# A convolution and two feed-forward layers in one kernel: layer 2 begins behind four blocks of layer 1, its weights are split at an even pace, TensorE's row halves start at unit 16

## The chip, the cores and the metric

The kernel runs on one core of a Trainium2 chip. Its time is the device time of one execution in microseconds (us). Before the change it is 2398.25 us, the median of three runs (2397.28 to 2398.75).

## What is computed

The inputs are x of 4 x 4096 x 192 (16384 tokens of 192 channels), 8 x 7 filter taps, and two pairs of weights, w_in of 192 x 2048 and w_out of 2048 x 192. The reference, cut to what matters:

```python
w = softmax(weight)                                   # 8 heads, 7 taps, each head 24 channels
x = causal convolution of x with w, head by head      # 16384 x 192
h = np.maximum(x @ moe_w_in, 0.0);  x = h * h @ moe_w_out                    # layer 1
h = x @ moe2_w_in
g = np.where(h > 0.0, h, np.exp(np.minimum(h, 0.0)) - 1.0);  out = g @ moe2_w_out   # layer 2
```

The weights arrive as 64-bit words (the kernel reads each as two 32-bit halves, `raw[..., 0]` and `raw[..., 1]`, and builds a float from them).

## The kernel before, in words

**Precision by splitting.** TensorE multiplies in a reduced format (float32r). So each operand, weights, inputs and the hidden values g, is held as a high part and a low part, and each product is three: high by high, low by high, high by low.

**Blocks and units.** Tokens are cut into 32 blocks of 512 (`NB`, `TB`). The 2048 hidden columns are 16 tiles of 128, taken two at a time: 8 pairs (`NP`). One *unit* is one layer, one block, one pair: 512 units in all. In the program's loop over u, TensorE does for unit u the products of x with w_in (`gemm1`, into the PSUM tile `h`), and for unit u - 3 (`LAG`) those of g with w_out (`gemm2`, into the PSUM tiles `y1A`, `y1B` or `y2A`, `y2B`). Between the two stand, for each unit: `r`, the relu of h by ScalarE (`act_first`); in layer 2 an exponential by ScalarE and then an operation of VectorE; the square in layer 1, by ScalarE up to unit 39; `gh`, the high part, by ScalarE (`finish_g`); `gl`, the low part, by VectorE or for five units by GpSimd (`finish_lo`).

**192 channels.** They are 128 ("A") and 64 ("B"). The B part of x fills only 64 of 128 rows, so the tokens' two halves lie in the two row halves, and each half of B is copied to the other row half as well (`move`, four DMAs a block, into `x1Bh` and `x1Bl`), since both halves of the array need it.

**Two ways of multiplying.** Before unit `HALVES` (32) a product is one instruction over 128 rows. From there on (`products` with halves) it is two instructions over 64 rows each, issued in pairs, half 0 and half 1 with different work, so that the two run together. The halves write to the same PSUM tile at different times, and SyncE's queue carries the signals between them (the no-operations in `products`, `SIGNALS` and `WAITS`): in this stage whatever is issued on that queue stands between signals, and so `later` puts a DMA off by two units.

**Order of the units.** `merge` interleaves block 0 of layer 1 with block 1, shifted by 3 units (units 0 to 15). Then block 2 of layer 1 is interleaved with block 0 of layer 2 (units 16 to 31). From unit 32 on come whole blocks: layer 2 block 1, layer 1 block 3, layer 2 block 2, layer 1 block 4, and so on.

**The weights in pieces.** Each layer's weights are cut into 18 pieces (`pieces`: six of A, four of B, eight of w_out, "o"), each with a unit at which it is due. `piece_step` works on three pieces at once: it ends an old one (`finish`: a copy by ScalarE or GpSimd and subtractions by GpSimd), begins a new one (`start`, `sign`, `guard`: a Square by ScalarE and three operations by VectorE), and does the middle of one (`power`, `rest`: two by VectorE, an addition by GpSimd), and then loads a further one by DMA into `raw`. So a step is five operations on VectorE. `more_pieces` makes up to two steps in a unit, as long as the piece is due within 8 units (4 for the last pieces), and `pieces_for` those that are due now. Each engine runs its instructions in program order, so a step stands on VectorE between one unit's `gl` and the next one's.

**The x side.** For each block `place_tasks` transposes x in, and `conv_tasks` applies 7 taps to the A part (`acc`, 128x512) and 7 to the B part (128x256) on VectorE, then splits the result (`hi_a`, `hi_b` on ScalarE, `lo_a`, `lo_b` on VectorE). For blocks 0 and 1 ("early") the B taps are ScalarE multiplications added up by GpSimd. These tasks wait in the list `bg`, which gives two or more to each unit; where a unit's block is not ready, the loop `while (layer, j) not in ready` takes all that is left at once.

Of the kernel before, what the change touches and what calls it, by code (L numbers as in the profile page):

```python
# [8 lines left out]
F32 = mybir.dt.float32  # L9
# [7 lines left out]
P = 128  # L17
TB = 512
# [4 lines left out]

LEAD = 3

HALVES = 32

AHEAD = (8, 4)

A_PIECES = ((0, 2), (2, 4), (4, 7), (7, 10), (10, 13), (13, 16))  # L30
B_PIECES = ((0, 2), (2, 4), (4, 6), (6, 8))
# [4 lines left out]
def f32(ap):  # L36
    return ap.bitcast(F32)
# [3 lines left out]
def conv_moe_moe_kernel(  # L41
# [34 lines left out]
    xt_p = ctx.enter_context(tc.tile_pool(name="xt", bufs=2))  # L76
    acc_p = ctx.enter_context(tc.tile_pool(name="acc", bufs=1))
    in_p = ctx.enter_context(tc.tile_pool(name="in", bufs=2))
    tmp_p = ctx.enter_context(tc.tile_pool(name="tmp", bufs=3))
    g_p = ctx.enter_context(tc.tile_pool(name="g", bufs=LAG))  # L80
    ev_p = ctx.enter_context(tc.tile_pool(name="ev", bufs=2))
    ps_h = ctx.enter_context(tc.tile_pool(name="ps_h", bufs=2, space=PSUM))
    ps_1 = ctx.enter_context(tc.tile_pool(name="ps_1", bufs=2, space=PSUM))
    ps_2 = ctx.enter_context(tc.tile_pool(name="ps_2", bufs=2, space=PSUM))


    cwA = cpool.tile([P, K], F32, name="cwA")
# [55 lines left out]
    class Piece:  # L143


        def __init__(self, layer, part, c0, c1):
            self.layer, self.part, self.c0, self.c1 = layer, part, c0, c1
            self.n = (c1 - c0) * (D if part == "o" else P)

        def load(self):  # L150
            wi, wo = w32[2 * (self.layer - 1) : 2 * self.layer]
# [166 lines left out]
    def conv_tasks(j, early=False):  # L318
        tasks = []
        st = {}  # L320

        def tap(i, cw, k):
            t = xT[j][i]
            n = (TB, HB)[i]
            if early and i == 1:
                c = acc_p.tile([P, n], F32, tag="acc1" if k == 0 else "tap", name="acc", bufs=1 if k == 0 else 2)
                nc.scalar.mul(out=c, in_=t[:, k : k + n], mul=cw[:, k : k + 1])
                if k == 0:
                    st[i] = c
                else:  # L330
                    nc.gpsimd.tensor_tensor(out=st[i], in0=st[i], in1=c, op=ALU.add)
            elif k == 0:
                st[i] = acc_p.tile([P, n], F32, tag=f"acc{i}", name="acc")
                nc.vector.tensor_scalar(out=st[i], in0=t[:, 0:n], scalar1=cw[:, 0:1], scalar2=None, op0=ALU.mult)
            else:
                nc.vector.scalar_tensor_tensor(  # L336
                    out=st[i], in0=t[:, k : k + n], scalar=cw[:, k : k + 1], in1=st[i], op0=ALU.mult, op1=ALU.add
                )

        def hi_a():  # L340
            X1[j] = in_tiles("x1")
            nc.scalar.copy(out=X1[j][0], in_=st[0])

        def lo_a():
            eng = nc.gpsimd if j in (1, 2) else nc.vector
            eng.tensor_tensor(out=X1[j][1], in0=st[0], in1=f32(X1[j][0]), op=ALU.subtract)

        def halves():
            return [(slice(s * DB, (s + 1) * DB), slice(s * HB, (s + 1) * HB)) for s in range(2)]

        def hi_b():
            for p, n in halves():
                nc.scalar.copy(out=X1[j][2][p, n], in_=st[1][p, :])

        def lo_b():
            h, l = X1[j][2:]
            for p, n in halves():
                nc.vector.tensor_tensor(out=l[p, n], in0=st[1][p, :], in1=f32(h[p, n]), op=ALU.subtract)


            def move(t, p, n, other):
                nc.sync.dma_start(out=f32(t[other, n]), in_=f32(t[p, n]))
                if t is l and other.start == 0:
                    ready.add((1, j))

            for t in (h, l):
                for (p, n), (other, _) in zip(halves(), reversed(halves())):
                    later(lambda t=t, p=p, n=n, other=other: move(t, p, n, other))

        for k in range(K):  # L370
            tasks.append(lambda k=k: tap(0, cwA, k))
            tasks.append(lambda k=k: tap(1, cwB, k))
        return tasks + [hi_a, hi_b, lo_a, lo_b]
# [19 lines left out]

    Y = {}

    def gemm2(layer, j, i, gh, gl):

        if i == 0:
            pool, tag = (ps_1, "y1") if layer == 1 and j != 1 else (ps_2, "y2")
            Y[layer, j] = [pool.tile([P, TB], F32, tag=tag, name=f"y{layer}{s}") for s in "AB"]  # L400
        o = (W1 if layer == 1 else W2)["o"]
        hi, lo, b = slice(0, P), slice(D + DB, 2 * D), slice(P, D + DB)
        todo = {
            "A": [(s, d, g) for s in range(2) for d, g in ((hi, gh), (lo, gh))] + [(s, hi, gl) for s in range(2)],
            "B": [(s, b, g) for g in (gh, gl) for s in range(2)],
        }
        work = {}
        for half in range(2):
            for y, part in zip(Y[layer, j], "AB"):
                begins = i == 0 and half == "AB".index(part)  # L410
                ends = i == NP - 1 and half != "AB".index(part)
                last = len(todo[part]) - 1
                work[half, part] = [
                    (o[:, 2 * i + s, d], g[:, s, :], y, begins and k == 0, ends and k == last)
                    for k, (s, d, g) in enumerate(todo[part])
                ]
        return work
# [57 lines left out]
    def fold_b(yB, n):  # L475

        t = ev_p.tile([P, TB], F32, tag="yt", name="yt", bufs=1)
        for d in range(0, n, DB):
            nc.scalar.copy(out=t[d : d + DB, :], in_=yB[DB - d : P - d, :])
        s = ev_p.tile([P, TB], F32, tag="ys", name="ys", bufs=1)  # L480
        nc.vector.tensor_tensor(out=s[0:n], in0=yB[0:n], in1=t[0:n], op=ALU.add)
        return s

    def y1_tasks(j):
        st = {}

        def split_to(hi, lo, src):
            nc.scalar.copy(out=hi, in_=src)
            nc.vector.tensor_tensor(out=lo, in0=src, in1=f32(hi), op=ALU.subtract)

        def a():
            X2[j] = in_tiles("x2")
            st["s"] = fold_b(Y[1, j][1], P)

        def b():
            split_to(X2[j][0], X2[j][1], Y.pop((1, j))[0])

        def c():
            split_to(X2[j][2], X2[j][3], st["s"])
            ready.add((2, j))  # L500

        return [a, b, c]

    def y2_tasks(j):

# [23 lines left out]
        return [unit for _, _, unit in sorted(at)]  # L529

    units = merge((1, 0, 0, 1.0), (1, 1, LEAD, 1.0))
    first_l2 = len(units)
    units += merge((1, 2, 0, 1.0), (2, 0, 0, 0.85))
    for j in range(3, NB):
        units += [(layer, b, c) for layer, b in ((2, j - 2), (1, j)) for c in range(NP)]
    units += [(2, j, c) for j in (NB - 2, NB - 1) for c in range(NP)]
    NU = len(units)
    at = {unit: u for u, unit in enumerate(units)}

    due, queue = zip(*(pieces(1) + pieces(2)))  # L540
    n_loaded = n_piece = 0

    def load_piece():
        nonlocal n_loaded
        if n_loaded < len(queue):
            queue[n_loaded].load()
            n_loaded += 1

    def piece_step():

        nonlocal n_piece
        i = n_piece
        new, mid, old = (queue[k] if 0 <= k < len(queue) else None for k in (i, i - 1, i - 2))
        if old:
            old.finish()
        if new:
            new.start()
        if mid:
            mid.power()
        if new:  # L560
            new.sign()
        if mid:
            mid.rest()
            load_piece()
        if new:
            new.guard()
        n_piece += 1
# [4 lines left out]
            piece_step()  # L572

    def more_pieces(u):
        ahead = AHEAD[n_piece >= len(queue) - 8]
        if n_piece < len(due) + 2 and due[max(n_piece - 2, 0)] <= u + ahead:
            piece_step()

    with tc.manual_schedule():
# [44 lines left out]
        def next_x(l2, j2, c2):  # L624

            if (l2, j2) == (1, 1):
                return {0: 2, 6: 3}.get(c2)
            if l2 == 2 and j2 and c2 == 2 and j2 + 3 < NB:
                return j2 + 3

        for u in range(NU + LAG):
            now = u
            pieces_for(u)
            if u < NU:
                layer, j, c = units[u]
                while (layer, j) not in ready:
                    bg.popleft()[1]() if bg else transfer()
                hs[u], first = gemm1(W1 if layer == 1 else W2, (X1 if layer == 1 else X2)[j], c)
# [22 lines left out]
            if 0 <= v:  # L661
                l2, j2, c2 = units[v]
                if c2 == NP - 1:
                    tasks = (y1_tasks if l2 == 1 else y2_tasks)(j2)
                    if v < first_l2 or (l2, 0) in [(n[0], n[2]) for n in units[v + 1 : v + 3]]:
                        for t in tasks:
                            t()
                    else:
                        bg.extendleft((0, t) for t in reversed(tasks))
                jx = next_x(l2, j2, c2)  # L670
                if jx:

# [42 lines left out]
```

## Time and profile before

| | |
|---|---|
| median of three runs | 2398.25 us |
| the profiled execution, its own time | 2400.75 us |
| its span, first to last instruction | 2399.0 us |
| mean granted TensorE clock, share of full | 0.988 |
| TensorE busy with matmuls | 2315.8 us (97%) |
| VectorE busy | 1746.5 us (73%) |
| ScalarE busy | 1489.1 us (62%) |
| GpSimd busy | 126.9 us (5%) |

The profile's 40 slices of the span are 60 us each. TensorE's busy share in tenths is 4, 7, 7, 8 in the first four and 9 in all that follow but the last (7). The granted clock is 8 or 9 tenths in the first four. GpSimd is busy in these four alone. TensorE's chain of matmuls makes up 82% of the chain that ended last. So the page has two parts: some 240 us in which TensorE waits now and then, and 2140 us in which it hardly does.

In the trace a unit is found by its first matmul into `h`. Unit 0's begins at 22.02 us, unit 16's at 136.62; unit 32, the first in halves, begins at 239.99.

### The profile page before, as it was taken

Reading aid. Unit: us, or ns where it says so; the run is one execution under the profiler, and the core shown is the slowest. Engines: PE = TensorE matmul, PEld = TensorE weight load, DVE = VectorE, ACT = ScalarE, POOL = GpSimd, SP = SyncE. Lnnn points to the kernel's source line nnn. Section 1 sums busy time; section 2 is a strip of 40 time slices with the busy share of each in tenths; the row PEclk is TensorE's granted clock in tenths of the full one; section 3 lists DMA queues with packets and bytes.
Section 4 is the critical chain, followed back from the end, with each engine's and each line's share of the span. In section 5 each row is a group of like instructions: output and inputs, shape, how many; then the busy total and the mean of one; then the engine's idle time right before and its main releaser. Section 6 shows DMA issues by size and latency. Waiting matters only on the chain.

```text
span 2399.0 us, 45460 instructions
## 1 busy us (share of the span) xinstructions
PE 2315.8 (97%) x18948; PEld 1935.1 (81%) x18948; DVE 1746.5 (73%) x2053; ACT 1489.1 (62%) x1641; POOL 126.9 (5%) x132
## 2 busy tenths in 40 slices
PE   4778999999999999999999999999999999999997
PEld 2555888888888888888888888888888889888886
DVE  7978677777777777777777777777777777777654
ACT  4656666656666656666666666665666666666664
POOL 5546000000000000000000000000000000000000
PEclk8989999999999999999999999999999999999998
DMA  3311100101000110100010100010010001010000
GB/s 87 85 48 42 16 16 13 19 16 17 17 15 13 18 18 16 19 12 15 16 19 15 19 15 15 13 19 17 17 18 13 14 17 19 14 19 5 12 8 14
DMA packets 222621, 49.08 MB, mean 20 GB/s; under 512 B 206545, under 2 KB 220881, under 8 KB 222417
## 3 DMA queue, kind: packets, MB, share of 16 engines
q1 hardware_dynamic: 221312, 46.05, 10.0%
q8 instruction: 150, 2.46, 0.4%
q14 instruction: 55, 0.44, 0.1%
q10 hardware_dynamic: 1104, 0.13, 0.1%
HBM read 25.17 MB, written 12.58 MB: 16 GB/s over the span
## 4 chain that ended last, share of the span: by engine, by line
PE 82%; DVE 8%; ACT 5%; issue 2%; SPq 1%; DMA 1%; POOL 0%; DVEq 0%; ACTq 0%
PE h L435 38%; PE y2A L435 13%; PE y1A L435 13%; PE y1B L435 8%; PE y2B L435 8%; ACT gh L611 2%; DVE r L471 2%; ACT r L458 1%; DVE gl L617 1%; DVE acc L336 1%; ACT r L462 1%; DVE a L176 1%; SPq L513 1%; DVE r L469 1%; DVE a L187 0%
## 5 line engine op out<-in xcount | busy, mean ns | idle before, releaser
L611 ACT CAST gh<-r 128x1024 fp32r<-128x1024 f32 x512 | 537.5, 1050 | 632.1 <-DVE r L469 322.5
L617 DVE TENSOR_TENSOR gl<-r,gh 128x1024 fp32r<-128x1024 f32 x507 | 625.9, 1235 | 339.1 <-ACT gh L611 339.1
L458 ACT ACTIVATE r<-h 128x1024 f32<-128x1024 f32 x512 | 524.1, 1024 | 180.3 <-PE h L435 155.7
L435 PE MATMUL y2A<-gh,wo 64*128 64x512 f32 x1968 | 539.2, 393 | 8.4 <-issue 7.6
L435 PE MATMUL y1A<-gh,wo 64*128 64x512 f32 x1872 | 511.7, 392 | 0.9 <-SPq L440 0.7
L471 DVE SCALAR_TENSOR_TENSOR r<-r,h 128x1024 f32<-128x1024 f32 x256 | 311.7, 1218 | 239.1 <-ACT r L462 216.4
L435 PEld LDWEIGHTS y2A<-gh,wo 64*128 64x128 f32 x1968 | 356.5, 185 | 39.1 <-issue 8.4
L435 PEld LDWEIGHTS y1A<-gh,wo 64*128 64x128 f32 x1872 | 338.0, 184 | 26.0 <-SPq L440 4.0
L469 DVE SCALAR_TENSOR_TENSOR r<-h,r 128x1024 f32<-128x1024 f32 x232 | 282.6, 1218 | 48.4 <-ACT r L458 47.8
L435 PE MATMUL h<-x2Ah,wiAh 64*128 64x512 f32 x992 | 311.6, 394 | 0.0
L435 PE MATMUL h<-x2Ah,wiAl 64*128 64x512 f32 x992 | 310.4, 392 | 0.0
L435 PE MATMUL h<-x2Al,wiAh 64*128 64x512 f32 x992 | 310.4, 393 | 0.0
L435 PE MATMUL y2A<-gl,wo 64*128 64x512 f32 x984 | 309.4, 394 | 0.0
L435 PE MATMUL y2B<-gh,wo 64*128 64x512 f32 x984 | 308.4, 393 | 0.0
L435 PE MATMUL y2B<-gl,wo 64*128 64x512 f32 x984 | 308.1, 392 | 0.0
L435 PE MATMUL y1B<-gl,wo 64*128 64x512 f32 x936 | 292.7, 392 | 0.3 <-DVE gl L617 0.3
L435 PE MATMUL y1B<-gh,wo 64*128 64x512 f32 x936 | 292.6, 392 | 0.0
L435 PE MATMUL y1A<-gl,wo 64*128 64x512 f32 x936 | 292.6, 392 | 0.0
L435 PE MATMUL h<-x1Ah,wiAl 64*128 64x512 f32 x928 | 290.1, 392 | 0.0
L435 PE MATMUL h<-x1Al,wiAh 64*128 64x512 f32 x928 | 290.0, 392 | 0.0
L435 PE MATMUL h<-x1Ah,wiAh 64*128 64x512 f32 x928 | 290.0, 392 | 0.0
L462 ACT ACTIVATE r<-r 128x1024 f32<-128x1024 f32 x256 | 271.5, 1061 | 7.8
(126 smaller groups left out, 4862.6 us busy)
## 6 DMA issues: line engine op xcount, KB each, us to landing
xinA<-in_x_dram SPq DMA_DIRECT2D x128, 64.0 KB, 2.3
out_dram<-zA SPq DMA_DIRECT2D x128, 64.0 KB, 2.0
raw<-in_moe_w_out_dram SPq DMA_DIRECT2D x16, 384.0 KB, 3.2
x1Bh<-x1Bh SPq DMA_DIRECT2D x64, 64.0 KB, 2.0
x1Bl<-x1Bl SPq DMA_DIRECT2D x64, 64.0 KB, 2.0
out_dram<-zB SPq DMA_DIRECT2D x64, 64.0 KB, 2.0
xinB<-in_x_dram SPq DMA_DIRECT2D x124, 32.0 KB, 2.0
raw<-in_moe_w_in_dram SPq DMA_DIRECT2D x8, 384.0 KB, 3.3
```

Of the source, the lines that this page charges most:

```text
L176: nc.vector.tensor_scalar(out=self.a.bitcast(U32), in0=hw, scalar1=3, scalar2=0x3FFFFFFF, op0=ALU.logical_shift_left, op1=ALU.bitwise_and,)
L336: nc.vector.scalar_tensor_tensor(out=st[i], in0=t[:, k : k + n], scalar=cw[:, k : k + 1], in1=st[i], op0=ALU.mult, op1=ALU.add)
L435: m = nc.tensor.matmul(o, w[p], x[p], start=st, stop=sp)
L458: nc.scalar.activation(out=r, in_=h, func=AF.Relu, scale=1.0 if layer == 1 else -1.0)
L462: nc.scalar.activation(out=r, in_=r, func=AF.Exp, scale=-1.0)
L469: nc.vector.scalar_tensor_tensor(out=r, in0=h, scalar=0.0, in1=r, op0=ALU.max, op1=ALU.mult)
L471: nc.vector.scalar_tensor_tensor(out=r, in0=r, scalar=-1.0, in1=h, op0=ALU.add, op1=ALU.max)
L513: later(lambda q=q, d=d: nc.sync.dma_start(out=dst[:, :, d : d + Q], in_=z[q * Q : (q + 1) * Q]))
L611: nc.scalar.copy(out=gh, in_=gs[u])
L617: eng.tensor_tensor(out=gl, in0=gs.pop(u), in1=f32(gsplit[u][0]), op=ALU.subtract)
```

## The change

It does six things. (1) The order of units 16 to 47: blocks 2 and 3 of layer 1 come whole, then blocks 0 and 1 of layer 2; from unit 48 on the order is what it was. (2) The halves begin at unit 16 instead of 32. (3) Layer 2's pieces begin at unit 13 and then one every 1.35 units (`begin`, `STEP`), instead of as early as 8 units ahead; `pieces_for` still forces a step where a piece is due, and the loads of pieces go through `later`. (4) For the early blocks 0 and 1 the other halves of x's B are written by ScalarE (`hi_b` copies twice, `lo_b` adds two copies) instead of by four DMAs. (5) The results of layer 1's blocks 2 and 3 are copied out of PSUM (`keep`, `HELD`) and split later, at units 40 and 48; the tasks at a block's end always go through `bg`. (6) The tile `r` has two buffers instead of three, and the four PSUM tiles of y come from one pool.

```diff
-HALVES = 32
-AHEAD = (8, 4)
+HALVES = 16
+AHEAD, STEP = 8, 1.35
...
-    tmp_p = ctx.enter_context(tc.tile_pool(name="tmp", bufs=3))
+    tmp_p = ctx.enter_context(tc.tile_pool(name="tmp", bufs=2))
-    ps_1 = ctx.enter_context(tc.tile_pool(name="ps_1", bufs=2, space=PSUM))
-    ps_2 = ctx.enter_context(tc.tile_pool(name="ps_2", bufs=2, space=PSUM))
+    ps_y = ctx.enter_context(tc.tile_pool(name="ps_y", bufs=4, space=PSUM))
...
         def hi_b():
-            for p, n in halves():
+            for (p, n), (other, _) in zip(halves(), reversed(halves())):
                 nc.scalar.copy(out=X1[j][2][p, n], in_=st[1][p, :])
+                if early:
+                    nc.scalar.copy(out=X1[j][2][other, n], in_=st[1][p, :])
         def lo_b():
...
+            if early:
+                for (p, n), (other, _) in zip(halves(), reversed(halves())):
+                    nc.scalar.copy(out=l[other, n], in_=f32(l[p, n]))
+                ready.add((1, j))
+                return
...
+        def fold():
+            st["s"] = fold_b(Y[1, j][1], P)
+        def keep():
+            st["a"] = ev_p.tile([P, TB], F32, tag="ya", name="ya", bufs=len(HELD))
+            nc.scalar.copy(out=st["a"], in_=Y.pop((1, j))[0])
...
+        if j in HELD:
+            held.append((at[2, j - 2, NP - 1] + 1, lambda: (a(), b())))
+            return [fold, keep]
+        return [fold, a, b]
...
-    first_l2 = len(units)
-    units += merge((1, 2, 0, 1.0), (2, 0, 0, 0.85))
-    for j in range(3, NB):
-        units += [(layer, b, c) for layer, b in ((2, j - 2), (1, j)) for c in range(NP)]
-    units += [(2, j, c) for j in (NB - 2, NB - 1) for c in range(NP)]
+    phases = [(1, 2), (1, 3), (2, 0), (2, 1)]
+    for j in range(4, NB):
+        phases += [(2, j - 2), (1, j)]
+    units += [(layer, j, c) for layer, j in phases + [(2, NB - 2), (2, NB - 1)] for c in range(NP)]
...
+    n1 = sum(p.layer == 1 for p in queue)
+    begin = [due[i] - AHEAD if i < n1 else 2 * NP - LAG + (i - n1) * STEP for i in range(len(due))]
...
-            queue[n_loaded].load()
+            later(queue[n_loaded].load)
...
+            while new.raw is None:
+                transfer()
             new.start()
...
-        ahead = AHEAD[n_piece >= len(queue) - 8]
-        if n_piece < len(due) + 2 and due[max(n_piece - 2, 0)] <= u + ahead:
+        if n_piece < len(due) + 2 and begin[min(n_piece, len(due) - 1)] <= u:
             piece_step()
...
+            if held and held[0][0] <= u:
+                bg.appendleft(held.popleft())
```

**VectorE, behind the `gl` of unit 5, before.** A group `a<-raw`, `m<-a`, `a<-raw,a`, `m<-raw,m`, `a<-m,a` is one piece step; `gl` is the low part of one unit's hidden values.

```order
L617 TENSOR_TENSOR gl<-r,gh 128x1024
L176 TENSOR_SCALAR a<-raw 128x384
L203 TENSOR_SCALAR m<-a 128x384
L187 SCALAR_TENSOR_TENSOR a<-raw,a 128x384
L210 SCALAR_TENSOR_TENSOR m<-raw,m 128x384
L198 SCALAR_TENSOR_TENSOR a<-m,a 128x384
L176 TENSOR_SCALAR a<-raw 128x256
L203 TENSOR_SCALAR m<-a 128x384
L187 SCALAR_TENSOR_TENSOR a<-raw,a 128x256
L210 SCALAR_TENSOR_TENSOR m<-raw,m 128x384
L198 SCALAR_TENSOR_TENSOR a<-m,a 128x256
L617 TENSOR_TENSOR gl<-r,gh 128x1024
```

The same place on VectorE after the change, down to the `gl` of unit 7:

```order
L636 TENSOR_TENSOR gl<-r,gh 128x1024
L177 TENSOR_SCALAR a<-raw 128x384
L204 TENSOR_SCALAR m<-a 128x384
L188 SCALAR_TENSOR_TENSOR a<-raw,a 128x384
L211 SCALAR_TENSOR_TENSOR m<-raw,m 128x384
L199 SCALAR_TENSOR_TENSOR a<-m,a 128x384
L636 TENSOR_TENSOR gl<-r,gh 128x1024
L294 COPY xtA<-xtA 128x6
L295 COPY xtB<-xtB 64x6
L304 STREAM_TRANSPOSE xtA<-xinA 128x512
L304 STREAM_TRANSPOSE xtB<-xinB 128x256
L306 COPY xtB<-xtB 64x6
```

The second step, the first of layer 2's pieces, is gone from here. Between the `gl` of units 5 and 14 there were eleven steps, and there are three.

**VectorE at unit 24, the first unit of layer 1's block 3, after.** The first row is the `gl` of unit 23, `acc` are taps of block 3, `x1Al` and `x1Bl` the low parts of that block's input, and the five rows that read or write `raw`, `a` and `m` are a piece step.

```order
L636 TENSOR_TENSOR gl_1524<-r_1518,gh_1522 128x1024
L337 SCALAR_TENSOR_TENSOR acc_1341<-xtA_1143,cwA_88,acc_1341 128x512
L177 TENSOR_SCALAR a_1535<-raw_1531 128x256
L204 TENSOR_SCALAR m_1464<-a_1465 128x384
L188 SCALAR_TENSOR_TENSOR a_1535<-raw_1531,a_1535 128x256
L211 SCALAR_TENSOR_TENSOR m_1464<-raw_1396,m_1464 128x384
L199 SCALAR_TENSOR_TENSOR a_1535<-m_1534,a_1535 128x256
L337 SCALAR_TENSOR_TENSOR acc_1401<-xtB_1144,cwB_89,acc_1401 128x256
```

Behind these follow six more taps, of A and B in turn, of which the last two stand here, and then the two low parts:

```order
L337 SCALAR_TENSOR_TENSOR acc_1341<-xtA_1143,cwA_88,acc_1341 128x512
L337 SCALAR_TENSOR_TENSOR acc_1401<-xtB_1144,cwB_89,acc_1401 128x256
L347 TENSOR_TENSOR x1Al_1551<-acc_1341,x1Ah_1550 128x512
L361 TENSOR_TENSOR x1Bl_1553<-acc_1401,x1Bh_1552 64x256 x2
L177 TENSOR_SCALAR a_1621<-raw_1560 128x384
```

All that is left of block 3's convolution now stands in one run ahead of unit 24's products, with a piece step in it. Before, block 3 was first needed at unit 40, and its taps stood one or two to a unit, for example

```order
L617 TENSOR_TENSOR gl_1394<-r_1343,gh_1391 128x1024
L336 SCALAR_TENSOR_TENSOR acc_1265<-xtB_1203,cwB_92,acc_1265 128x256
L336 SCALAR_TENSOR_TENSOR acc_1219<-xtA_1202,cwA_91,acc_1219 128x512
L176 TENSOR_SCALAR a_1402<-raw_1315 128x384
L203 TENSOR_SCALAR m_1355<-a_1356 128x384
```

behind the `gl` of unit 20; their number in a unit has not changed, but the unit by which they must be done has.

## Rows read from the trace of the kernel before

**Rows 1.** TensorE's waits, 0 to 245 us: who waited for whom, total, times, longest.

```profile
PE h L448 <- ACT r L458: 12.4, 5, 3.4
PE h L454 <- DMA x1Bh<-x1Bh: 8.8, 3, 5.3
PE h L448 <- POOL x1Al L346: 6.8, 1, 6.8
PE h L448 <- DVE r L471: 6.6, 3, 2.8
```

**Rows 2.** Timeline of TensorE: start, length, what; in brackets idle before, releaser.

```profile
32.07 0.89 PE L454 MATMUL h<-x1Bh,wiBh 64*128 64x512 f32 x2 [3.05 <-DMA x1Bh<-x1Bh]
...
94.54 0.63 PE L448 MATMUL y1B<-gl,wo 128*128 128x512 f32 x2
96.60 0.50 PE L448 MATMUL h<-x1Ah,wiAh 128*128 128x512 f32 x1 [1.43 <-ACT r L458]
...
136.62 0.40 PE L448 MATMUL h<-x1Ah,wiAh 128*128 128x512 f32 x1
...
153.10 2.07 PE L448 MATMUL y1A<-gh,wo 128*128 128x512 f32 x4
...
160.14 1.20 PE L448 MATMUL y1A<-gh,wo 128*128 128x512 f32 x4
...
162.57 0.39 PE L448 MATMUL h<-x2Ah,wiAh 128*128 128x512 f32 x1
...
167.38 0.40 PE L448 MATMUL h<-x1Ah,wiAh 128*128 128x512 f32 x1
...
239.99 0.50 PE L435 MATMUL y2A<-gh,wo 64*128 64x512 f32 x1
```

**Rows 3.** The chain that ended last, two neighbouring units in halves.

```profile
295.44 1.40 PE h L435 x12
299.87 1.40 PE h L435 x12
```

**Rows 4.** Timeline of ScalarE.

```profile
21.93 0.83 ACT L353 CAST x1Bh<-acc 64x256 fp32r<-64x256 f32 x2
...
33.84 1.02 ACT L458 ACTIVATE r<-h 128x1024 f32<-128x1024 f32 x1 [6.74 <-PE h L454]
...
94.79 0.51 ACT L221 CAST wo<-a 128x384 fp32r<-128x384 f32 x1 [3.48 <-POOL a L213]
```

**Rows 5.** Timeline of VectorE.

```profile
38.05 0.75 DVE L198 SCALAR_TENSOR_TENSOR a<-m,a 128x384 f32<-128x384 f32 x1 [4.23 <-ACT m L175]
...
108.44 0.47 DVE L336 SCALAR_TENSOR_TENSOR acc<-xtB,cwB,acc 128x256 f32<-128x256 f32 x1
108.84 0.74 DVE L336 SCALAR_TENSOR_TENSOR acc<-xtA,cwA,acc 128x512 f32<-128x512 f32 x1
109.50 0.28 DVE L176 TENSOR_SCALAR a<-raw 128x256 uint32<-128x256 uint32 x1
...
110.91 0.35 DVE L176 TENSOR_SCALAR a<-raw 128x384 uint32<-128x384 uint32 x1
...
173.72 2.92 DVE L336 SCALAR_TENSOR_TENSOR acc<-xtA,cwA,acc 128x512 f32<-128x512 f32 x1
```

**Rows 6.** Timeline of GpSimd.

```profile
173.68 2.40 POOL L617 TENSOR_TENSOR gl<-r,gh 128x1024 fp32r<-128x1024 f32 x1 [16.07 <-ACT gh L611]
```

**Rows 7.** A stretch's busy time: us, PE, PEld, DVE, ACT, POOL, clock, DMA.

```profile
68.00:93.80 25.80, 17.93 (x71) 11.63 (x71) 24.87 (x37) 13.66 (x21) 15.78 (x17) 0.93 0.27 82
```

**Rows 8.** The costliest groups: count, then busy us, mean ns of one.

```profile
L617 DVE TENSOR_TENSOR gl<-r,gh 128x1024 fp32r<-128x1024 f32 x507 | 625.9, 1235 | 339.1 <-ACT gh L611 339.1
```

**Rows 9.** DMA issues: count, KB each, median us from issue to landing.

```profile
x1Bh<-x1Bh SPq DMA_DIRECT2D x64, 64.0 KB, 2.0
```

**Rows 10.** Waits of SyncE's queue.

```profile
SPq L155 <- DVE m L210: 59.7, 15, 9.5
```

More of the change, by code (lines that the diff above doesn't have):

```diff
@@ L148, in __init__ @@
             self.n = (c1 - c0) * (D if part == "o" else P)
+            self.raw = None
         def load(self):
@@ L394, in conv_moe_moe_kernel @@
     Y = {}
+    HELD = (2, 3)
+    held = deque()
     def gemm2(layer, j, i, gh, gl):
         if i == 0:
-            pool, tag = (ps_1, "y1") if layer == 1 and j != 1 else (ps_2, "y2")
-            Y[layer, j] = [pool.tile([P, TB], F32, tag=tag, name=f"y{layer}{s}") for s in "AB"]
+            Y[layer, j] = [ps_y.tile([P, TB], F32, tag="y", name=f"y{layer}{s}") for s in "AB"]
         o = (W1 if layer == 1 else W2)["o"]
@@ L479, in fold_b @@
             nc.scalar.copy(out=t[d : d + DB, :], in_=yB[DB - d : P - d, :])
-        s = ev_p.tile([P, TB], F32, tag="ys", name="ys", bufs=1)
+        s = ev_p.tile([P, TB], F32, tag="ys", name="ys", bufs=len(HELD))
         nc.vector.tensor_tensor(out=s[0:n], in0=yB[0:n], in1=t[0:n], op=ALU.add)
@@ L489, in split_to @@
             nc.vector.tensor_tensor(out=lo, in0=src, in1=f32(hi), op=ALU.subtract)
+        def fold():
[3 more added lines that the diff above has]
+            nc.scalar.copy(out=st["a"], in_=Y.pop((1, j))[0])
         def a():
             X2[j] = in_tiles("x2")
-            st["s"] = fold_b(Y[1, j][1], P)
+            split_to(X2[j][0], X2[j][1], st["a"] if j in HELD else Y.pop((1, j))[0])
         def b():
-            split_to(X2[j][0], X2[j][1], Y.pop((1, j))[0])
-        def c():
             split_to(X2[j][2], X2[j][3], st["s"])
             ready.add((2, j))
-        return [a, b, c]
+        if j in HELD:
+            held.append((at[2, j - 2, NP - 1] + 1, lambda: (a(), b())))
+            return [fold, keep]
+        return [fold, a, b]
     def y2_tasks(j):
@@ L627, in next_x @@
                 return {0: 2, 6: 3}.get(c2)
-            if l2 == 2 and j2 and c2 == 2 and j2 + 3 < NB:
-                return j2 + 3
+            if l2 == 2 and c2 == 2 and j2 != 1:
+                return 4 if j2 == 0 else j2 + 3 if j2 + 3 < NB else None
         for u in range(NU + LAG):
@@ L664, in conv_moe_moe_kernel @@
                     tasks = (y1_tasks if l2 == 1 else y2_tasks)(j2)
[L665 to L669, printed above, removed]
+                    bg.extendleft((0, t) for t in reversed(tasks))
                 jx = next_x(l2, j2, c2)
```

## The prediction

> **What bounds the kernel now.** I read first the page's slices: TensorE is full from about 240 us on and not before. Two neighbouring units in the late part begin 299.87 - 295.44 = 4.43 us apart [rows 3], the pace of the pairs of half-height matmuls; the 480 units behind 239.99 us at that pace make 2126 of the remaining 2159 us. Nothing in that part is touched, so what can be gained lies ahead of 239.99 us. Then the list of TensorE's waits there [rows 1]: for ScalarE's relu (12.4 us), for the DMA copies of x's B (8.8), for block 2's low part from GpSimd (6.8), for VectorE's layer-2 operation (6.6). Then the timelines, to see what stands behind these waits: VectorE is busy for 24.87 of 25.80 us while the first weights are split [rows 7], and ScalarE's relu stands behind a copy that waits for GpSimd's addition, which waits for VectorE (3.48 us in one case, [rows 4]). So the beginning is bound by the splitting of weights, in whose shadow TensorE is busy for seven tenths of the time.
>
> Unit 16 begins at 136.62 and unit 32 at 239.99 [rows 2]: 103.4 us for 16 units, where the late pace would need 70.9.
>
> **The change part by part.** I keep a ledger of TensorE's start of units 16 and 32.
>
> *Early copies.* Unit 0 waited 3.05 us for a DMA of x's B [rows 2]. ScalarE now does two more copies of the high part, then two of the low part; two such copies take 0.83 us [rows 4], and the low ones end before TensorE has done unit 0's A products. The relu of unit 0 had ScalarE waiting for TensorE for 6.74 us [rows 4], and VectorE waited 4.23 us for a Square queued behind it [rows 5], so the 3.05 us pass on to VectorE, the bound of this stage. Block 1 costs four copies as well, 1.66 us, on ScalarE ahead of weight copies, with no TensorE wait to gain. Bounds: -3.05 and, if nothing passes on, +1.7. I take -2.4, near the first, since VectorE's wait is on the chain.
>
> *Layer 2's pieces later.* Between the low parts of units 5 and 14 VectorE loses eight of eleven steps. With the first goes the copy that waited 3.48 us [rows 4] ahead of unit 7's relu, on which unit 9's start waited (1.43 us, [rows 2]). Unit 8's last products begin at 94.54 and are 0.47 long by the starts of their neighbours, so unit 9 begins at 95.0 instead of 96.60. From there I take seven units back to back at 167.38 - 162.57 = 4.81 us [rows 2]: unit 16 at 128.7 instead of 136.62, **-7.9**. VectorE has room for that: per unit one `gl` of 1.24 [rows 8] and two taps (0.40 and 0.66 by their starts, [rows 5]). It cannot be more, since TensorE is then without gaps; it can be 0 if another wait stands in the same place (the last two w_out pieces of layer 1 are now finished only in the units that need them). I take the whole.
>
> *Units 16 to 31, all of layer 1 and in halves.* 16 x 4.43 = 70.9 us if TensorE never waits. Layer 1 has no VectorE operation that reads h, so the 6.6 us of waits for that go. What is late next:
>
> - Unit 16 needs block 2's B. Behind unit 15's h stand on ScalarE a relu, a `gh` and a Square at 1.02 each [rows 4], a copy half as large (0.5) and the two copies of x1Bh (0.83): 4.4. Then VectorE's low parts (as long, 0.8), then four DMAs one after the other on SyncE's queue (an estimate of 1 us for the issue of the last two) and 2.0 to land [rows 9]: 8.2 us. TensorE has work for 2.4 us (unit 12's gemm2, 160.14 to 162.57) and some eight pairs, 1.9 us. Stall **4**, where before 6.8 and 5.3 us were lost [rows 1].
> - Unit 24 needs block 3, and all that is left of its convolution is taken there at once. From the end of unit 23's products: relu, Square and `gh` 3.1; `gl` 1.24; a tap 0.66; a piece step 1.41 (109.50 to 110.91, [rows 5]); seven taps, four B and three A, 3.6; the copies of x1Bh behind the last 0.83; low parts 0.8; the DMAs 3.0. Together 14.6. That step's `raw` is loaded only in the same unit, behind x loads, and GpSimd works beside VectorE: I add 2. TensorE has some eight pairs, 1.9 us, to do. Stall **15**; 8 if VectorE is ahead of this, 22 if each step in it meets GpSimd.
> - After such a gap matmuls are slow: four took 2.07 us at 153.10 and 1.20 at 160.14 [rows 2], the lower of the clock's two levels (1.2 GHz) against the upper. Some 6 us of work at half pace cost **3**, as they did before behind unit 16's gap.
> - Steps whose `raw` lands late, and the handing over from whole to half height: **2**, between 0 and 6.
>
> 94.9 us instead of 103.4: **-8.5**, with ends of -22 and +10.
>
> *VectorE in units 16 to 31.* Twelve steps at 1.41 (256 columns) to an estimated 1.75 (384 columns, by the 0.28 and 0.35 of a step's first operation, [rows 5]), twelve `gl` at 1.24, a block's taps (7.4) and some 5 us of transposes and splits: 46 us beside 70.9. GpSimd's part of these steps is two to four instructions of 0.93 (15.78 / 17, [rows 7]), some 2.5 us a step, and it makes five `gl` of 2.40 [rows 6]: 42 us. The two get in each other's way: a tap of 0.74 took 2.92 us [rows 5] while GpSimd made a `gl` from 173.68 to 176.08 [rows 6]. How much in the mean: in the stretch of rows 7, 34 step operations (a fifth of 1.75 each) and three `gl` are 16 us of work, VectorE was busy for 24.87, GpSimd for 15.78, so VectorE loses a little over half of GpSimd's time. Units 16 to 23 hold seven `gl` (8.7), six steps (9.5) and 7 us of taps, transposes and splits, 25 us, beside 20 of GpSimd (six steps, two `gl`). With half they need 35 us on VectorE, and TensorE 35.4: just covered, and I cost it at nothing beyond the 2 above.
>
> The Trainium skill's GPSIMD Engine Reference (section 1, Specifications) says that GpSimd shares its SBUF interfaces with VectorE and contends with VectorE instructions that have two SBUF inputs. The tap above has two, and its 2.92 us agree; were VectorE stopped for all of GpSimd's time, the result would be the second rival below, and rows 7 speak for half.
>
> *Units 32 to 36.* Four of layer 2's steps fall into units of layer 2, where VectorE has two operations of 1.24 and a step with GpSimd beside it: 2.5 + 1.75 + 1.25 = 5.5 against 4.43. TensorE waits once its two h buffers are used up: **+2**, between 0 and 6. Before, these units were free of steps.
>
> *Two buffers of r, one pool for y, copies kept for blocks 2 and 3.* The relu of unit u now waits for the `gl` of unit u - 2. In the halves that `gl` ends some 4.3 us behind its relu, in units 7 to 15 some 8, and the relu comes at 8.9 or 9.6, so nothing; if VectorE lags by over 2 us it costs what it lags, which is in the bounds above. `keep` adds two copies of 0.5 on ScalarE at units 27 and 35; layer 1 needs 3.1 of 4.43 there. Cost 0.
>
> Sum: -2.4 - 7.9 - 8.5 + 2 = **-16.8 us**. The profiled execution took 2400.75 us, so 2384; it is 2.5 above the median of the runs, so I forecast **2381.5 us**.
>
> **The rivals.** *The gap at unit 24 is small.* For it: the same kind of wait at unit 16 cost 6.8 and 5.3 us [rows 1], not 15. Against: at unit 16 no taps were left. If the stall is 8 and without its slow clock, -10 more: 2371.5.
>
> *VectorE becomes the bound of units 16 to 31.* If GpSimd's time stops VectorE in full, units 16 to 23 need 25 + 20 = 45 us instead of 35.4 and units 25 to 31 18 + 20 = 38 instead of 31: +17, and the change is worth nothing, 2398.5. For it speaks the tap of 2.92 us, against it the half of rows 7, and that layer 1's units leave VectorE only the `gl`.
>
> *SyncE's queue holds TensorE.* This is the one on the other side. From unit 16 on the weight loads stand between the signals of the halves. Before, such a load waited 59.7 / 15 = 4.0 us for VectorE to be done with the buffer [rows 10]. TensorE can go on for ten pairs, 2.3 us, without the next signal. Fourteen loads follow; if each still waits that long, they cost 14 x 1.7 = 24 us: 2405.5, slower. It decides once VectorE is more than a unit behind. Against it: a load is put off by two units (8.9 us), and the operation that it waits for comes in the step of its own unit.
>
> **How the numbers follow.** Forecast 0.53, with its own range of 2374 to 2391; small gap 0.2; VectorE as the bound 0.14; SyncE's queue 0.1; something else 0.03. Leaving out the far side of the small gap and nearly all of SyncE's rival, 8 in 10 lie between 2365 and 2400. A measurement of this kernel can tell 0.2% from no change, that is 4.8 us. Faster takes the forecast, the small gap and a share of the second rival: 0.80. The same is most of the rest of that rival: 0.08. Slower: 0.12.
>
> **What would show it.** In the profile after: unit 0's B products without a DMA wait, its relu at 31 us; unit 9 to 15 at 4.8 us each and unit 16 at 126 us; a gap of 4 us in unit 16; then 4.4 us a unit; a gap of 13 to 16 us at unit 24, released by the copy of block 3's A and then by DMAs of its B, with a lower granted clock behind it; unit 32 at about 221 us. I am wrong if unit 24 comes without a gap, if units 17 to 23 take over 5 us each with VectorE full, or if TensorE waits for SyncE.

## The result, and the profile after

In its first runs the changed kernel takes 2377.25 us (median of three, 2375.77 to 2378.87) against 2397.87 us before; run again it takes 2374.37 us (median of four, 2372.28 to 2374.74) against 2398.37 us before, a ratio of 0.9898 [0.9885, 0.9912]. That is 20.6 and 24.0 us less, where 16.8 were forecast; below, "the changed kernel" is the second set of runs. One more execution of the changed kernel, its first profiled one, was disturbed (5327.65 us), so every line "after" below is from its next profiled execution: 2372.28 us, span 2370.5 us, mean granted clock 0.992.

TensorE's waits after, 0 to 245 us (who waited for whom, total, times, longest), answer to [rows 1]:

```profile
...
PE h L444 <- ACT x1Ah L343: 12.5, 1, 12.5
PE h L457 <- ACT r L467: 6.2, 4, 2.4
...
PE y1A L457 <- POOL wo L225: 3.0, 5, 0.9
PE h L444 <- DVE r L480: 2.3, 2, 1.3
```

The waits for block 2's low part (6.8) and most of those for DMAs of x's B (8.8) are gone; there is one new gap of 12.5 us, and five short waits for w_out's low parts (3.0, before 1.1 in two), of which the last two, 0.18 and 0.41 us, are for pieces that are now ended only in the units that need them. TensorE's timeline (start, length, what, in brackets idle before and releaser) answers to [rows 2]:

```profile
28.92 0.79 PE L463 MATMUL h<-x1Bh,wiBh 64*128 64x512 f32 x2
...
95.63 0.40 PE L457 MATMUL h<-x1Ah,wiAh 128*128 128x512 f32 x1
...
100.45 0.39 PE L457 MATMUL h<-x1Ah,wiAh 128*128 128x512 f32 x1
...
126.76 0.40 PE L444 MATMUL h<-x1Ah,wiAh 64*128 64x512 f32 x1
...
129.19 0.47 PE L444 MATMUL h<-x1Bh,wiBh 64*128 64x512 f32 x1 [1.35 <-DMA x1Bh<-x1Bh]
...
130.42 0.47 PE L444 MATMUL h<-x1Bl,wiBh 64*128 64x512 f32 x1 [0.19 <-DMA x1Bl<-x1Bl]
...
177.76 0.79 PE L444 MATMUL h<-x1Ah,wiAh 64*128 64x512 f32 x1 [12.47 <-ACT x1Ah L343]
...
180.10 0.76 PE L444 MATMUL h<-x1Bh,wiBh 64*128 64x512 f32 x1 [0.69 <-DMA x1Bh<-x1Bh]
```

Unit 0's B products wait for nothing, units 10 and 11 begin 4.82 us apart, unit 16's first matmul into `h` is at 126.76 us and the unit hardly waits, and unit 24 has the gap, behind which matmuls take 0.6 to 0.8 us instead of 0.39. The stretches (us, PE, PEld, DVE, ACT, POOL, clock, DMA), to be held against [rows 7]:

```profile
133.00:166.00 33.00, 32.29 (x277) 31.00 (x273) 25.41 (x39) 30.11 (x38) 16.81 (x12) 1.00 0.18 43
166.00:187.00 21.00, 8.54 (x49) 7.07 (x51) 14.26 (x27) 5.62 (x9) 3.99 (x3) 0.67 0.24 66
187.00:222.00 35.00, 35.00 (x304) 35.00 (x302) 25.15 (x29) 28.63 (x36) 20.89 (x19) 1.00 0.16 47
222.00:255.00 33.00, 26.94 (x225) 22.31 (x221) 26.84 (x39) 20.55 (x25) 14.96 (x20) 1.00 0.13 44
```

TensorE is full in units 17 to 23 and 25 to 31; the granted clock of the stretch with the gap is 0.67, between its two levels (1.2 and 2.4 GHz); and from 222 us on, in the first units of layer 2, 6 us are lost again.

The gain is best followed by the start of each unit's relu on ScalarE (read from ScalarE's timeline, as in [rows 4]):

| unit | before | after | difference |
|---|---|---|---|
| 0 | 33.84 | 30.50 | -3.3 |
| 16 | 153.20 | 133.14 | -20.1 |
| 24 | 198.01 | 185.05 | -13.0 |
| 32 | 244.73 | 221.49 | -23.2 |
| 44 | 298.81 | 283.24 | -15.6 |
| 504 | 2345.62 | 2326.67 | -19.0 |
| 508 | 2372.80 | 2344.20 | -28.6 |

The last step, 9.7 us more between units 504 and 508, was in no term of the forecast. The rows for it are in the trace of before, TensorE's and then VectorE's timeline:

```profile
2352.73 0.39 PE L435 MATMUL h<-x2Al,wiAh 64*128 64x512 f32 x1
2360.75 0.76 PE L435 MATMUL y2A<-gh,wo 64*128 64x512 f32 x1 [7.64 <-issue]
2361.36 0.76 PE L435 MATMUL y2B<-gh,wo 64*128 64x512 f32 x1
```

```profile
2359.94 0.71 DVE L510 STREAM_TRANSPOSE zA<-y2A 128x512 f32<-128x512 f32 x1
```

Before, TensorE stands for 7.64 us at the first y product of the last block. The profile names no engine ("issue"), but TensorE goes on 0.1 us after VectorE's transpose of y2A has ended. The tile is the clue: the last two blocks are both layer 2, and before the change they draw y2A and y2B from a pool of two tiles, and so the last block waits until the one ahead of it is stored.

The stretch of 460 units between 44 and 504 took 2046.8 us before and 2043.4 after. In the other profiled executions below it lies between these two (2043.5 to 2046.3). So up to 3.4 us of a comparison of two traces can come from that stretch, where no term of the forecast lies; what makes it longer or shorter is not shown.

### The profile page after: what moved, and what is told of

It is laid out like the page before. It is cut to its first block, busy times and chain, and to the rows that moved or that the text cites. A ratio compares the mean times of both kernels' runs of the same rounds, so it can differ in the third digit from the quotient of the medians.

```text
span 5325.9 us, 46051 instructions
## 1 busy us (share of the span) xinstructions
PE 5283.7 (99%) x19204; PEld 5033.4 (95%) x19204; DVE 1738.7 (33%) x2045; ACT 1527.4 (29%) x1659; POOL 117.6 (2%) x132
## 4 chain that ended last, share of the span: by engine, by line
PE 99%; DVE 1%; DMA 0%; ACT 0%; POOL 0%; issue 0%; SPq 0%; DVEq 0%; ACTq 0%
PE h L444 45%; PE y2A L444 15%; PE y1A L444 15%; PE y2B L444 10%; PE y1B L444 10%; PE y1A L457 1%; PE h L457 1%; PE y1B L457 1%; PE h L463 0%; DVE acc L337 0%; PE y2A L457 0%; DMA raw<-in_moe_w_in_dram 0%; PE y2B L457 0%; DVE a L177 0%; ACT r L467 0%
## 5 line engine op out<-in xcount | busy, mean ns | idle before, releaser
L444 PE MATMUL y2A<-gh,wo 64*128 64x512 f32 x2024 | 1204.0, 758 | 0.0
L444 PE MATMUL y1A<-gh,wo 64*128 64x512 f32 x1944 | 1159.6, 760 | 0.0
L444 PE MATMUL y2B<-gl,wo 64*128 64x512 f32 x1012 | 657.5, 759 | 0.0
L444 PE MATMUL y2B<-gh,wo 64*128 64x512 f32 x1012 | 657.1, 758 | 0.0
L444 PE MATMUL y2A<-gl,wo 64*128 64x512 f32 x1012 | 656.9, 758 | 0.0
L444 PE MATMUL h<-x2Al,wiAh 64*128 64x512 f32 x1024 | 655.5, 758 | 0.0
L444 PE MATMUL h<-x2Ah,wiAl 64*128 64x512 f32 x1024 | 655.5, 759 | 0.0
L444 PE MATMUL h<-x2Ah,wiAh 64*128 64x512 f32 x1024 | 654.8, 758 | 0.0
L444 PE MATMUL y1A<-gl,wo 64*128 64x512 f32 x972 | 633.5, 761 | 0.0
L444 PE MATMUL h<-x2Bl,wiBh 64*128 64x512 f32 x512 | 380.9, 756 | 0.0
```

Source lines behind the costliest of these rows:

```text
L444: m = nc.tensor.matmul(o, w[p], x[p], start=st, stop=sp)
```

## The experiments

**The changed kernel once more.** No edit.

> The changed kernel as it is, for a trace at the usual pace of TensorE (in the execution that was profiled first every matmul took about 2.3 times its usual time, for reasons outside the program). My ledger: about 2377 us; unit 16 starts at about 126 us, unit 24 has a gap of 13 to 16 us ended by ScalarE's copy of block 3's A and by the DMAs of its B, unit 32 starts at about 221 us. If VectorE bounds units 16 to 31, these take over 5 us each without one large gap. If SyncE's queue holds TensorE, TensorE's waits name SyncE.

Measured: 2374.37 us, ratio 0.9898 [0.9885, 0.9912]; its trace is the "after" above. The gap at unit 24 is there with 12.5 us, so the rival of a small gap falls. VectorE was busy for 25.41 of 33 us in units 17 to 23, so the rival of VectorE as the bound falls. From unit 16 to 245 us, where the weight loads are, TensorE never waits for SyncE, and behind that for 0.2 us in all, so the third rival falls for this kernel.

**The early copies undone.** Blocks 0 and 1 use the DMAs again (`early` parts of `hi_b` and `lo_b` taken out).

```diff
-                if early:
-                    nc.scalar.copy(out=X1[j][2][other, n], in_=st[1][p, :])
...
-            if early:
-                for (p, n), (other, _) in zip(halves(), reversed(halves())):
-                    nc.scalar.copy(out=l[other, n], in_=f32(l[p, n]))
-                ready.add((1, j))
-                return
```

> The changed kernel, but the other halves of x's B of blocks 0 and 1 are moved by four DMAs each as before. If unit 0's wait of 3 us passes on through VectorE, this is 2.4 us slower than the changed kernel, some 2379.5. If ScalarE's extra copies cost what they save, it is the same, 2377.

Measured: 2376.16 us (2374.24 to 2377.98), ratio 0.9907 [0.9894, 0.9921]: 1.8 us by the medians, with intervals that overlap; 2.7 us at unit 6 and 3.1 at the last unit in the traces.

**The early copies alone**, in the kernel before (the same lines added there).

> The kernel before with the early copies alone: the other halves of x's B of blocks 0 and 1 are written by ScalarE instead of DMAs. The prediction took -2.4 us (between -3.05 and +1.7); undone in the changed kernel it was worth 1.8 us. Theory A (what unit 0 gains is on the path of VectorE's splitting, and is kept): the relu of unit 16 some 2.5 us earlier, 2396 us, ratio 0.999. Rival B (in the order before, block 2's low part and DMAs hold unit 16 anyway): within 0.5 us of the kernel before.

Measured: 2395.75 us, ratio 0.9988 [0.998, 0.9997]; the relu of unit 16 at 150.49 instead of 153.20. Theory A: what unit 0 gains is kept. The gap at the end is there too, 7.60 us: the second execution that has it, of another program with two pools.

**One pool for y**, in the kernel before. No instruction is added or moved, only waits change.

```diff
-    ps_1 = ctx.enter_context(tc.tile_pool(name="ps_1", bufs=2, space=PSUM))
-    ps_2 = ctx.enter_context(tc.tile_pool(name="ps_2", bufs=2, space=PSUM))
+    ps_y = ctx.enter_context(tc.tile_pool(name="ps_y", bufs=4, space=PSUM))
...
-            pool, tag = (ps_1, "y1") if layer == 1 and j != 1 else (ps_2, "y2")
-            Y[layer, j] = [pool.tile([P, TB], F32, tag=tag, name=f"y{layer}{s}") for s in "AB"]
+            Y[layer, j] = [ps_y.tile([P, TB], F32, tag="y", name=f"y{layer}{s}") for s in "AB"]
```

> The kernel before with one change: the PSUM tiles of y come from one pool of four instead of two pools of two; no instruction is added or moved. In the trace of before TensorE stands still for 7.64 us at 2353.1, between the last two blocks, and goes on 0.1 us after VectorE's transpose of y2A (2359.94, 0.71 long); the matmuls behind it are at the lower clock; units 504 to 508 take 27.2 us instead of 17.5. Theory A (the last block, layer 2 behind layer 2, waits for the two tiles of the block ahead of it, and four tiles take this wait away): no gap there, 8 to 10 us less, 2389 us, ratio 0.996. Rival B (the gap belongs to that one profiled execution, or to the supply of instructions late in the program): 2398 us, ratio 1.000, and the gap is seen again or not whatever the pools are.

Measured: 2389.89 us (2389.16 to 2392.05), ratio 0.9964 [0.9952, 0.9977], 9.0 us less. The stretch around the end of this kernel has TensorE full and the clock at its upper level:

```profile
2340.00:2362.00 22.00, 22.00 (x192) 18.41 (x190) 13.23 (x13) 15.85 (x16) 0.00 (x0) 1.00 0.01 1
```

Theory A is shown: the gap was the pool, and this part of the change alone is worth some 9 of its 24 us. In the traces nearly all of it lies where the gap was: from unit 504 to unit 508 it takes 18.4 us instead of 27.2.

**Halves from unit 32 on**, in the changed kernel.

```diff
-HALVES = 16
+HALVES = 32
```

> The changed kernel, but TensorE's row halves begin at unit 32 again. If TensorE's pace sets units 16 to 31 outside the gap at unit 24, each of 15 units costs 4.81 instead of 4.43: 6 us more, some 2383. If VectorE or the gap bounds them, it is the same, 2377.

Measured: 2379.2 us (2377.45 to 2381.57), ratio 0.9922 [0.9909, 0.9934]: 4.8 us by the medians. In the traces it is more: from the relu of unit 16 to that of unit 32 it takes 96.8 us instead of 88.4. Part of that is not the height: unit 16 waits longer for its DMAs (2.6 us instead of 1.35), and behind it the granted clock is lower (0.91 from 130 to 166 us). The gap at unit 24 is 9.5 instead of 12.5; units 16 to 21 take longer (33.4 us instead of 26.6), which leaves the convolution more time.

**Layer 2's pieces as early as unit 6**, one every half unit, in the changed kernel.

```diff
-    begin = [due[i] - AHEAD if i < n1 else 2 * NP - LAG + (i - n1) * STEP for i in range(len(due))]
+    begin = [due[i] - AHEAD if i < n1 else 6 + (i - n1) * 0.5 for i in range(len(due))]
```

> The changed kernel, but layer 2's pieces begin at unit 6 and come one every half unit, so up to two in a unit, about as they did before the change; order, halves and copies as changed. If the later pieces are what lets units 9 to 15 run at TensorE's pace, unit 16 starts 8 us later, of which 3 come back since units 16 to 36 are then free of steps: some 2382. If the steps only move the same work about, it is the same, 2377.

Measured: 2412.22 us, ratio 1.0057 [1.0044, 1.0071]: 38 us more. The sign was as expected, the size was not: this puts all eighteen steps of layer 2 ahead of unit 16, where before ten stood there. TensorE's waits from 85 to 270 us, and the fullest stretch of VectorE:

```profile
PE h L457 <- ACT r L467: 18.9, 7, 4.3
PE h L444 <- POOL x1Al L347: 16.5, 1, 16.5
PE h L444 <- ACT x1Ah L343: 8.1, 1, 8.1
PE y1A L444 <- ACT gh L630: 7.8, 1, 7.8
```

```profile
125.00:150.00 25.00, 19.12 (x72) 11.97 (x72) 23.97 (x40) 12.19 (x17) 17.79 (x14) 0.86 0.28 82
```

VectorE is busy for 23.97 of 25 us, TensorE waits for the relu in seven units, and block 2's low part stands on GpSimd behind the steps (16.5 us at unit 16). Unit 16's relu comes 51 us later; 7.8 us come back in units 32 to 44, which are free of steps. So putting all steps that early loses more than the whole change gains; how much of the gain the pacing alone makes in the order of before was not tried.

**Block 3's convolution earlier**, in the changed kernel: its transposes and taps are begun at the third unit of block 1 and not the seventh.

```diff
-                return {0: 2, 6: 3}.get(c2)
+                return {0: 2, 2: 3}.get(c2)
```

> The changed kernel (2374.4 us), with block 3's transposes and taps begun four units of block 1 earlier: block 1's third unit starts them instead of its seventh, so that on VectorE all taps and block 3's A are done ahead of unit 24. Theory A (the gap at unit 24, 12.5 us and some 4 of slow clock, is the convolution left over there): no wait for x1Ah; what stays are the last DMAs of x1Bl, 2 to 4 us; 10 to 14 us less, 2362 us, ratio 0.985. Rival B (VectorE has no room in units 16 to 23 beside GpSimd): units 16 to 23 become 0.6 to 1.5 us longer each and the gap only moves; 2370 us, ratio 0.988.

Measured: 2364.86 us (2363.33 to 2366.24), ratio 0.9858 [0.9844, 0.9871]: 9.5 us less than the changed kernel. Its waits from 158 to 177 us:

```profile
PE h L444 <- DVE x1Al L347: 3.2, 1, 3.2
PE h L444 <- DMA x1Bh<-x1Bh: 1.4, 1, 1.4
PE h L444 <- DMA x1Bl<-x1Bl: 1.2, 1, 1.2
```

Theory A: 12.5 us became 3.2 and two short waits for DMAs, and the units ahead of it did not become longer (from the relu of unit 16 to that of unit 22 26.6 us in both). So the gap was the convolution left over at unit 24, as the prediction had built it up. Not all of the gain is from there: 2.3 us come already at unit 16 (its relu at 130.83 instead of 133.14), whose short waits for DMAs are gone too. With block 3's tasks the list `bg` is longer than 16 in some units ahead of unit 16, so the program takes four tasks in them and not two, and block 2's convolution ends sooner (its last tap starts at 111.9 us instead of 116.1).

**Steps faster**: one every unit, in the changed kernel, and the same with block 3's convolution early.

```diff
-AHEAD, STEP = 8, 1.35
+AHEAD, STEP = 8, 1.0
```

> The changed kernel with a step of layer 2's pieces every unit instead of every 1.35 units: the last step falls at unit 32 instead of 37. Units 32 to 44 took 61.75 us in the changed kernel, against 53.2 at the pace of the halves and 54.08 before. Theory A (the loss of 7.6 us there is VectorE's overload by four steps in units of layer 2): units 32 to 44 back to 55, 4 to 6 us less, 2369.5 us, ratio 0.988. Rival B (units 16 to 31 have no room for five more steps on VectorE): the gap at unit 24 or the units around it become longer by what is saved behind; 2374 to 2378 us, ratio 0.990 to 0.992.

> The changed kernel with both: block 3's taps begun four units of block 1 earlier, and a step every unit. If the two losses are independent: the sum of both gains, 2357 us, ratio 0.983. If VectorE fills up in units 16 to 24, with seven units of taps, a low part and a step in each: no better than the better one of the two alone, 2362 to 2368 us.

Measured: 2378.49 us, ratio 0.9915 [0.9901, 0.9928], and 2369.95 us, ratio 0.9878 [0.9863, 0.9893]: 4.1 and 5.1 us slower than with 1.35 (4.4 and 6.1 us at unit 44 in the traces). Both theories hold a part. Units 32 to 44 take 56.35 us instead of 61.75, the 5.4 us that theory A wanted; but ahead of them more is lost, in the first of the two kernels at these places:

```profile
PE h L444 <- ACT x1Ah L343: 13.7, 1, 13.7
PE h L444 <- POOL x1Al L347: 3.8, 1, 3.8
PE y1A L444 <- SPq L449: 2.9, 1, 2.9
```

Unit 16 now waits for block 2's low part on GpSimd, whose steps begin sooner (its relu comes at 137.88 instead of 133.14), and unit 24 waits longer. The third line is new: TensorE waits for a signal on SyncE's queue. In the second kernel that is the wait at unit 16; TensorE's line, and then one of SyncE's queue:

```profile
PE y1A L444 <- SPq L449: 4.4, 2, 4.1
```

```profile
SPq L168 <- DVE m L211: 8.8, 2, 7.2
```

For 7.2 us a weight load stood on the queue until VectorE was done with its buffer, and the signal behind it came 4.1 us too late for TensorE. That is the third rival's mechanism: it does not hold the changed kernel, but a step every unit brings it about.

**Faster only behind unit 24**: early convolution, 1.35 units a step up to the ninth step and 1 from there on; in the second kernel block 3 is also begun one unit of block 1 earlier (`1: 3`).

```diff
+    pace = lambda k: k * STEP if k <= 8 else 8 * STEP + (k - 8)
-    begin = [due[i] - AHEAD if i < n1 else 2 * NP - LAG + (i - n1) * STEP for i in range(len(due))]
+    begin = [due[i] - AHEAD if i < n1 else 2 * NP - LAG + pace(i - n1) for i in range(len(due))]
```

> Block 3's taps early as in the kernel of 2364.86 us, and layer 2's pieces every 1.35 units up to the ninth, from then on every unit: the steps of units 13 to 23 stay where they were, and two steps fewer fall into units of layer 2 (the last one goes from unit 37 to unit 34). Theory A (the loss behind unit 32 is VectorE's overload there, and what a step every unit spoiled was ahead of unit 24): units 32 to 44 go from 61.75 us towards 56.4, as they did with a step every unit, and nothing is lost ahead; -4, 2361 us, ratio 0.984. Rival B (units 24 to 31 have no room for the steps either): units 24 to 32 go from 36.5 us to 39 or more, 2364 us or slower.

> As the run before it, and block 3's taps one more unit of block 1 earlier, so that its low part of A stands behind one step less. Theory A: of the 5.8 us that TensorE still waits at unit 24 for block 3's low part of A and the DMAs of B, 1 to 2 go; 2359.5 us. Rival B: the steps and taps of units 16 to 23 fill VectorE, and it stays within 2 us of the run before it, 2361 to 2363 us.

Measured: 2362.98 us (2362.11 to 2363.3), ratio 0.9854 [0.9839, 0.9869], and 2364.88 us, 0.9865 [0.9851, 0.9878]. Theory A falls: units 32 to 44 take 60.4 us, against 61.75. Nor is it rival B: units 24 to 32 take 37.3 us, not 39. The loss only moved, from units 36 to 38 (12.7 us, now 8.7) to units 34 to 36 (now 12.8). The second is 1.5 us ahead of the first at unit 16 and 3.2 behind it at unit 24. The early convolution with either pace, 2363 to 2365 us, beats both kernels; the paces cannot be told apart.

**What was not tried alone.** The new order of the units, the copies kept (`keep`) and the two buffers of `r` were only run together with the rest, and the even pace not in the order of before. So the runs price three parts, the early copies (about 2 us), the halves (4.8 by the medians) and the pool (9.0); how the rest is shared out is not shown.

## Why the prediction was nearly right

*Early copies, -2.4.* Confirmed: 1.8 and 2.2 us by the medians of two pairs of kernels (the second clear of noise), 2.7 and 2.8 at unit 6 in their traces.

*Layer 2's pieces later, unit 16 at 126.3.* Unit 15's last products are followed by unit 16's at 125.72 us; in halves a unit's first matmul into `h` stands four pairs behind its start, here at 126.76 (of unit 32 before, 239.99 is the start). So the time is right, but two errors partly cancel. Unit 9 begins at 90.82, 1.8 us before the forecast's 92.6 (95.0 less 2.4). The seven units from there take 34.9 us instead of 33.7: four at 4.81 or 4.82 and one at 4.90, but two at 5.26 and 5.49, with the waits of 0.18 and 0.41 us for w_out's low parts that the forecast named and put at nothing.

*Units 16 to 31, 94.9 us.* The mechanism held and the sizes were too large. The stall at unit 16 is 1.35 + 0.19 us where 4 was taken; the gap at unit 24 is 12.5 + 0.7 where 15 was; the slow clock behind it was sized about right (six us of matmuls at 0.62 instead of 0.39). At unit 32 the change is 23.2 us ahead, not 18.8. The estimate that VectorE needs 35 us for units 16 to 23 was too high: it is busy for 25.41 of the 33 us ahead of the gap, and part of that work lies in the gap itself.

*VectorE overload behind unit 32, +2 with bounds 0 and 6.* The place is right, the term was too small: units 32 to 44 take 61.75 us instead of 54.08, 7.7 more, beyond the bound. VectorE's timeline from one `r` to the next with a step, after:

```profile
240.59 1.22 DVE L480 SCALAR_TENSOR_TENSOR r<-r,h 128x1024 f32<-128x1024 f32 x1
242.92 1.46 DVE L636 TENSOR_TENSOR gl<-r,gh 128x1024 fp32r<-128x1024 f32 x1 [1.11 <-ACT gh L630]
244.30 0.35 DVE L177 TENSOR_SCALAR a<-raw 128x384 uint32<-128x384 uint32 x1
...
245.78 0.55 DVE L199 SCALAR_TENSOR_TENSOR a<-m,a 128x384 f32<-128x384 f32 x1
246.25 1.21 DVE L480 SCALAR_TENSOR_TENSOR r<-r,h 128x1024 f32<-128x1024 f32 x1
```

and the same place in the run with the pieces early, where units 32 to 44 have no step and take 53.95 us:

```profile
283.94 1.22 DVE L480 SCALAR_TENSOR_TENSOR r<-r,h 128x1024 f32<-128x1024 f32 x1 [1.45 <-ACT r L471]
286.27 1.23 DVE L636 TENSOR_TENSOR gl<-r,gh 128x1024 fp32r<-128x1024 f32 x1 [1.11 <-ACT gh L630]
288.29 1.22 DVE L480 SCALAR_TENSOR_TENSOR r<-r,h 128x1024 f32<-128x1024 f32 x1 [0.79 <-ACT r L471]
```

With the step it is 5.66 us, without it 4.35. The forecast's 5.5 was near, but by luck: it put 1.25 us down to GpSimd, which costs 0.23 here (the `gl` of 1.46), and left out that VectorE idles 1.11 us between `r` and `gl`, since the high part on ScalarE waits for `r`. By its own durations alone, `r`, `gl` and a step of 1.75, VectorE would need 4.2 us, less than 4.43; the chain over two engines is what takes longer. The term was too small for two other reasons. Behind the fourth step stand the two operations that are left of the last piece, a fifth step that the forecast did not count: from 246.25 to the next `r` it is 7.54 us. And the two h buffers took up little: TensorE waited four times for `r`, since `r` frees the h tile, 0.97, 1.34, 0.95 and 2.84 us.

*One pool for y, 0.* This is the step that failed. "Two buffers of r, one pool for y, copies kept: ... Cost 0" looked for what the pool could cost and not for what it could give, and the opening said that nothing behind 239.99 us is touched. The pool touches the last block. The page of before had the wait, among the costliest groups:

```profile
L435 PE MATMUL y2A<-gh,wo 64*128 64x512 f32 x1968 | 539.2, 393 | 8.4 <-issue 7.6
```

and the opening's own sum, 2126 of 2159 us, left 33 us behind 239.99 unexplained, of which the wait and the slow clock behind it are part. The pool is worth 9.0 us, measured alone in the kernel before. At unit 44 the changed kernel was 15.6 us ahead, the forecast's sum was 16.8; without this term the time would have been some 2 us above the forecast of 2381.5, and with it it is 7.1 below (4.3 by the first runs). That the sum at unit 44 came so near is partly luck: 4.4 us too little gain up to unit 32 and 5.7 too little loss behind it are errors of opposite sign.

*The rivals.* Small gap, VectorE as the bound, SyncE's queue: all three were refuted for the changed kernel by the trace after, as said above. The last two are near: with all steps early VectorE is full (23.97 of 25 us), and with a step every unit SyncE's queue holds TensorE for 2.9 and 4.1 us.

## What to carry to other kernels

An idle stretch that the profile puts down to "issue" may be a tile pool that has run out: look at which tile the first instruction behind it writes, and which other engine last read that tile before it went on. When a change merges pools, list every pair of neighbouring blocks that drew from the same pool before, the last pair too, even if the rest of that part of the program is untouched. And cost work that is put between two steps of a chain over several engines by the length of the chain, not by the sum on one engine.

## What was not expected of the hardware

VectorE and GpSimd do not slow each other evenly. In the cases below, an instruction of VectorE that begins while GpSimd works ends behind GpSimd's by nearly its own usual length. After, GpSimd's timeline and then VectorE's:

```profile
226.83 1.48 POOL L234 TENSOR_TENSOR wiBl<-a,wiBh 128x256 fp32r<-128x256 f32 x1 [2.00 <-ACT wiBh L233]
...
240.25 1.24 POOL L214 TENSOR_TENSOR a<-a,m 128x384 f32<-128x384 f32 x1 [7.37 <-DVE m L211]
...
242.13 1.16 POOL L225 TENSOR_TENSOR wo<-a,wo 128x128 fp32r<-128x128 f32 x2
```

```profile
227.62 0.91 DVE L177 TENSOR_SCALAR a<-raw 128x384 uint32<-128x384 uint32 x1
```

GpSimd's first instruction ends at 228.31 and VectorE's at 228.53, 0.22 after it; it is 0.91 long instead of 0.35. GpSimd's last ends at 243.29, and the `gl` that began at 242.92 (shown above) ends at 244.38, that is 1.09 after it, where one alone takes 1.23. The tap of [rows 5] that took 2.92 us began 0.04 us behind the start of GpSimd's `gl` of [rows 6] and ended 0.56 us behind its end, where one alone takes 0.74. In these three cases VectorE's instruction looks as if it waited for GpSimd's to end. Not every one does: the `r` that began at 240.59 (shown above), with GpSimd's addition at work since 240.25, took its usual 1.22; of its two inputs one, h, lies in PSUM. The Trainium skill's SBUF — State Buffer (section "SBUF: two separate sides") says that the port pair that VectorE and GpSimd share is an exclusive lock: of a GpSimd instruction and a VectorE instruction that runs in a two-port mode or, where GpSimd's reads SBUF, has two SBUF inputs, whichever starts first has it for the whole instruction and the other is blocked. The `gl` and the tap, with two SBUF inputs, agree, and so does the `r`, with one; the first case has one SBUF input too, and no run here shows in which mode it ran. By the same rule GpSimd is blocked in turn, which would fit that over a longer stretch VectorE lost only half of GpSimd's time [rows 7]; no run here measured that by itself.
